# Query rows and output rows with the weights as moving operand, in a decode-attention and GLU backward kernel

## The chip, the cores and the metric

The kernel runs on one core of one Trainium2 chip. The metric is the device time of one execution in microseconds (us). A kernel's number is the median of several executions; executions of one kernel mostly lie within 0.3% of each other. A profile is one of these executions with the hardware profiler's records; its "span", from the first to the last instruction, is about 1.8 us shorter than the time. Engines are written PE (tensor engine; PEld is its weight load), DVE (vector), ACT (scalar), POOL (GpSimd) and SP (the queue that issues the large transfers). The granted clock is the share of its full clock that PE got, the DMA share the mean busy share of the 16 DMA engines; PSUM is the memory that PE writes its sums to.

## The reference

The program is one decode step, one token, with 32 heads and a cache of 8192 positions, plus a gated MLP, and the gradient of all of it. Cut to what matters:

```python
def _fwd_reference(A_x, A_k_cache, A_v_cache, A_wq, A_wo, B_x, B_w1, B_w3, B_w2):
    # x is 1 x 640; K and V are 32 heads x 8192 x 128; F of the MLP is 1728
    xn = _layernorm(x)
    q = xn @ wq                       # 4096 = 32 heads x 128
    p = softmax(q . k * Dh**-0.5)
    o = p . v
    return x + o @ wo + (silu(xn @ w1) * (xn @ w3)) @ w2

def reference(..., grad_out):
    _out, _vjp = jax.vjp(_f, A_x, A_k_cache, A_v_cache, A_wq, A_wo, B_w1, B_w3, B_w2)
    return (_out, *_vjp(grad_out))    # out_0, and out_1 = dx, dK, dV, dwq, dwo, dw1, dw3, dw2
```

K and V are read once (134 MB together) and gradients of the same size are written once. Nearly all the rest is the weights and their gradients. Each byte is used in a handful of operations.

## The kernel before

Heads are worked in groups of four (`GH = 4`), with one load of `wq` and `wo` per group. The 2 MB blocks of K and V live in ten buffers. A gradient is written into the buffer of the block that it belongs to, stored, and the buffer then takes a new load:

```python
    def store(kind, h):
        t = kv_tiles.pop((kind, h))
        ...
        fifo((dkc if kind == "K" else dvc)[h], t[:])    # 2 MB store on the SP queue
        free_slots.append(t)
        load_next()                                     # the next 2 MB load, into a freed buffer
```

These are the parts that the change touches. First q of a group, as columns: the weights are the stationary operand and one column of `xn` moves, 20 matmuls of one column.

```python
    def prep_q(g, ps, first):
        for hh in range(GH):
            for ci in range(NC):                        # NC = 5 blocks of 128 rows of D = 640
                nc.tensor.matmul(ps[:, hh:hh + 1], lhsT=G_["wq"][:, ci, hh * DH:(hh + 1) * DH],
                                 rhs=xn_col_bf[:, ci:ci + 1], ...)
        nc.scalar.activation(G_["cb"][:, 0, :], ps, ACTF.Copy, scale=scale)
```

Then the sum for `out_0`, again with the weights stationary: 20 matmuls of one column for each group, and 70 in the MLP (14 blocks of F by 5). The dx sum of the MLP lies in the same PSUM bank, `acc`, until the end.

```python
    acc = ps_acc.tile([P, 512], F32, name="acc")
    dx_acc = acc[:, 0:NC * RX].rearrange("p (c r) -> p c r", r=RX)
    OUT0 = NC * RX
    ...                                                 # fin_pe(g), once per group
            for ci in range(NC):
                nc.tensor.matmul(acc[:, OUT0 + ci:OUT0 + ci + 1], lhsT=G_["wo"][:, hh, ci * P:(ci + 1) * P],
                                 rhs=G_["od_bf"][:, hh, 0:1], ...)
    ...                                                 # mlp(), once, before head 2
            for ci in range(NC):
                nc.tensor.matmul(acc[:, OUT0 + ci:OUT0 + ci + 1], lhsT=wsrc[0:rows, ci * P:(ci + 1) * P],
                                 rhs=hcol_bf[0:rows, b:b + 1], ...)
    ...                                                 # the broadcasts of the MLP's gradient rows come next
    ...                                                 # the end
    nc.vector.tensor_reduce(dxm[:], dx_acc, AX.X, ALU.add)
    nc.vector.tensor_tensor(fin[:, 0:NC], acc[:, OUT0:OUT0 + NC], x_col[:], ALU.add)
    ...                                                 # fin is transposed, cast and stored by four small DMAs
```

## Time and profile before

| what | before | where it is read |
|---|---|---|
| time | 732.5 us, 732.12 to 733.51 in 3 runs | runs |
| span of the profile | 730.6 us | head of the page |
| PE, DVE, ACT busy | 83%, 63%, 51% | part 1 |
| moved | 303.58 MB, 416 GB/s on average | DMA line |
| matmuls (each with its weight load) | 5669 | part 1 |

The strips show what no average tells: the DMA engines are at 9 tenths or more in all slices but the last. The chain of work that ended last, by engine, looks otherwise:

```profile
PE 42%; DMA 41%; DVE 8%; ACT 6%; issue 1%; SPq 0%; ACTq 0%; DVEq 0%
```

This chain follows, at each step, whatever released the step last. A store frees a buffer, a load fills it, the tensor engine works on it, a store leaves: the walk passes through compute on a path that lies beside a full DMA pipe.

### The profile page before, as it was taken

What the parts mean: (1) busy time and instruction counts of PE and PEld (TensorE: products, weight loads), DVE (VectorE), ACT (ScalarE), POOL (GpSimd) and SP (SyncE); (2) the same over time, 40 slices, a digit from 0 to 9 for tenths busy, and PEclk for the clock granted to TensorE, in tenths of its full rate; (3) what the DMA queues carried; (4) which work ended last, traced back from release to release, by engine and by line L of the source; (5) the groups of instructions that cost most, each with busy time, mean ns of one, the idle gap of its engine ahead of it and who ended that gap; (6) DMA issues with size and microseconds to landing.
All of it is one profiled execution on the core that took longest, in us unless ns stands there. A gap on an engine that the chain in (4) does not pass through costs nothing.

```text
span 730.6 us, 13869 instructions
## 1 busy us (share of the span) xinstructions
PE 606.6 (83%) x5669; PEld 423.1 (58%) x5669; DVE 459.3 (63%) x806; ACT 369.4 (51%) x719; POOL 29.9 (4%) x45
## 2 busy tenths in 40 slices
PE   3989589998899889988987887888898889978940
PEld 2657466666566656666655555566566556655620
DVE  4069646677757776776646765547756756667482
ACT  2650736656556556554655554545554536655510
POOL 0010110000100000001000000000000000000000
PEclk9996699999999999988998998979897969989765
DMA  9999999999999999999999999999999999999993
GB/s 354 400 411 420 425 421 432 415 429 425 417 416 426 429 427 421 430 428 426 425 428 426 431 423 427 429 428 428 427 424 429 429 427 428 428 434 426 425 393 155
DMA packets 27145, 303.58 MB, mean 416 GB/s; under 512 B 2807, under 2 KB 4153, under 8 KB 10441
## 3 DMA queue, kind: packets, MB, share of 16 engines
q1 hardware_dynamic: 21328, 276.39, 89.5%
q0 software_dynamic: 5728, 26.30, 8.9%
q8 instruction: 44, 0.72, 0.4%
q14 instruction: 21, 0.16, 0.1%
q10 hardware_dynamic: 24, 0.01, 0.0%
HBM read 151.34 MB, written 151.34 MB: 414 GB/s over the span
## 4 chain that ended last, share of the span: by engine, by line
PE 42%; DMA 41%; DVE 8%; ACT 6%; issue 1%; SPq 0%; ACTq 0%; DVEq 0%
DMA out_dram<-kv 22%; PE pT L305 20%; DMA kv<-in_A_k_cache_dram 11%; DMA kv<-in_A_v_cache_dram 7%; PE m L340 6%; PE X L417 5%; ACT KT L307 4%; PE sA L324 4%; DVE kv L450 3%; PE dA L324 2%; DMA wo_g<-in_A_wo_dram 2%; DVE side L251 1%; PE gu_ps L527 1%; ACT KT L330 1%; PE m L430 1%
## 5 line engine op out<-in xcount | busy, mean ns | idle before, releaser
L307 ACT COPY KT<-pT 128x512 f32<-128x512 f32 x512 | 289.5, 589 | 235.3 <-PE pT L305 200.6
L305 PE MATMUL pT<-ident_f,kv 128*128 128x128 f32 x2048 | 318.7, 296 | 40.6 <-DMA kv<-in_A_k_cache_dram 17.9
L305 PEld LDWEIGHTS pT<-ident_f,kv 128*128 128x128 f32 x2048 | 248.5, 154 | 97.0 <-PE pT L305 27.8
L450 DVE TENSOR_TENSOR kv<-qd,U 128x4096 bf16<-128x4096 bf16 x64 | 146.0, 2284 | 0.0
L450 DVE TENSOR_TENSOR kv<-qd,P 128x4096 bf16<-128x4096 bf16 x64 | 143.6, 2284 | 0.0
L340 PEld LDWEIGHTS m<-selc,KT 128*128 128x128 f32 x512 | 67.4, 205 | 45.8 <-ACT KT L330 34.1
L340 PE MATMUL m<-selc,KT 128*128 128x16 f32 x512 | 73.2, 276 | 22.7 <-ACT KT L330 22.5
L417 PE MATMUL X<-kv,Z 128*32 128x512 bf16 x1024 | 85.3, 462 | 1.8 <-DVE Z L434 1.8
L400 DVE SCALAR_TENSOR_TENSOR U<-m,P 128x64 bf16<-128x64 f32 x32 | 7.4, 233 | 104.9 <-PE m L340 104.9
L324 PE MATMUL dA<-KT,qz 128*32 128x512 bf16 x512 | 55.2, 418 | 0.2 <-ACT KT L307 0.2
L324 PE MATMUL sA<-KT,qz 128*32 128x512 bf16 x512 | 55.1, 421 | 0.0
L324 PEld LDWEIGHTS <-qz 128*32 128x32 bf16 x1024 | 26.6, 93 | 42.8 <-issue 41.6
L417 PEld LDWEIGHTS <-Z 128*32 128x32 bf16 x1024 | 28.6, 110 | 33.9 <-issue 16.6
L366 DVE TENSOR_REDUCE mrow<-m 128x1 f32<-128x64 f32 x32 | 7.1, 223 | 62.9 <-PE m L340 62.9
L360 ACT CAST qd<-pT 128x256 bf16<-128x256 f32 x32 | 11.9, 372 | 48.6 <-DVE kv L450 32.4
L500 DVE SCALAR_TENSOR_TENSOR wq_g<-wq_g,side 128x512 bf16<-128x512 bf16 x40 | 27.3, 683 | 0.0
L251 DVE SCALAR_TENSOR_TENSOR side<-wo_g,g_bc 128x640 bf16<-128x640 bf16 x32 | 26.2, 819 | 1.1 <-DMA wo_g<-in_A_wo_dram 0.8
L373 DVE TENSOR_REDUCE negM<-m 128x1 f32<-128x128 f32 x32 | 9.3, 291 | 24.5 <-PE m L370 24.5
L432 DVE SCALAR_TENSOR_TENSOR U<-m,P 128x128 bf16<-128x128 f32 x32 | 11.4, 355 | 18.0 <-PE m L430 18.0
L390 DVE RECIPROCAL rZ<-m 128x1 f32<-128x1 f32 x32 | 5.3, 167 | 24.1 <-PE m L384 24.1
L330 ACT COPY KT<-dA 128x512 f32<-128x512 f32 x32 | 19.3, 604 | 0.6 <-PE dA L324 0.6
L330 ACT COPY KT<-sA 128x512 f32<-128x512 f32 x32 | 19.3, 603 | 0.0
(154 smaller groups left out, 365.2 us busy)
## 6 DMA issues: line engine op xcount, KB each, us to landing
out_dram<-kv SPq DMA_DIRECT2D x64, 2048.0 KB, 31.1
kv<-in_A_k_cache_dram SPq DMA_DIRECT2D x32, 2048.0 KB, 25.2
kv<-in_A_v_cache_dram SPq DMA_DIRECT2D x32, 2048.0 KB, 26.3
out_dram<-wo_g POOLq DMA_DIRECT2D x8, 640.0 KB, 11.4
out_dram<-wq_g POOLq DMA_DIRECT2D x8, 640.0 KB, 12.9
wq_g<-in_A_wq_dram POOLq DMA_DIRECT2D x7, 640.0 KB, 13.2
wo_g<-in_A_wo_dram POOLq DMA_DIRECT2D x7, 640.0 KB, 19.3
kv<-in_B_w_dram SPq DMA_DIRECT2D x2, 1728.0 KB, 28.7
```

Source lines behind the costliest of these rows:

```text
L251: nc.vector.scalar_tensor_tensor(junk[:], G_["wo"][:, hh, :], 1.0, g_bc[:], ALU.mult, ALU.mult, accum_out=G_["do"][:, hh:hh + 1])
L305: nc.tensor.transpose(pT[:, k * P:(k + 1) * P], W3[:, 4 * c + k, :], ident_f[:])
L307: nc.scalar.copy(KT[:].rearrange("p k w -> p (k w)"), pT[:])
L324: nc.tensor.matmul(S_[kind][q:q + QW, :], lhsT=S_["qz"][:, o:o + QW], rhs=KTb[:, par, :], start=(c0 == 0), stop=(c0 == NCH - 2), skip_grou ...
L330: nc.scalar.copy(XS[:].rearrange("p k w -> p (k w)"), S_.pop(kind)[:])
L340: nc.tensor.matmul(S_["m"][:, b0:b0 + J].rearrange("p (c k t) -> p k c t", k=4, t=2)[:, k, :, :], lhsT=XS[:, k, :], rhs=selc[:].rearrange( ...
L360: nc.scalar.copy(qd[:].rearrange("p a d -> p (a d)"), hd[h].pop("ps_r"))
L373: nc.vector.tensor_reduce(S_["negM"][:], S_["m"][:, 2 * J:2 * J + P], AX.X, ALU.max, negate=True)
L417: nc.tensor.matmul(xg["X"][q:q + QW, :], lhsT=Z[:, o:o + QW], rhs=W[:, N4 * i:N4 * (i + 1)], start=(slot == 0 and i < 4), stop=(slot == NS ...
L432: nc.vector.scalar_tensor_tensor(S_["U2"][:], S_["V"][:, 0:J].unsqueeze(2).to_broadcast([P, J, 2]), S_["m"][:, OC + NS:OC + NS + 1], S_["P ...
L450: nc.vector.tensor_tensor(dst[:, lo * DH:hi * DH].rearrange("p (j a b) -> p j a b", a=DH // 2, b=2), vec.rearrange("p (a b) -> p a b", b=2 ...
L500: nc.vector.scalar_tensor_tensor(wq_g[:, ci, :], wq_g[:, ci, :], 1.0, dqb, ALU.mult, ALU.mult, accum_out=dxa[:, ci, g:g + 1])
```

## The change

The intent was fewer and wider matmuls. The weights become the moving operand, 512 or 320 columns at a time, and a broadcast vector is stationary. `q` and `out_0` then come out as rows. Five wide matmuls and four one-column ones replace 20 for q, and 8 replace 20 for `out_0` per group; the MLP's 70 become 28 plus six that add `x`. dx of the MLP moves to a bank of its own and is reduced at once, the MLP's small vectors move into an unused tail of a buffer, and `out_0` leaves as two row stores. The core of the diff:

```diff
-    dx_acc = acc[:, 0:NC * RX].rearrange("p (c r) -> p c r", r=RX)
-    OUT0 = NC * RX
+    DHALF = D // 2
+
+    def out_row(vec, mat):
+        k = mat.shape[0]
+        for e in range(2):
+            nc.tensor.matmul(acc[64 * e:64 * (e + 1), 0:DHALF], lhsT=vec.to_broadcast([k, 64]),
+                             rhs=mat[:, e * DHALF:(e + 1) * DHALF], start=False, stop=True, skip_group_check=True)
...
-    def prep_q(g, ps, first):
+    def prep_q(g):
         G_ = grp[g]
+        pq = pst()
+        for ci in range(NC):
+            nc.tensor.matmul(pq[:], lhsT=xn_col_bf[:, ci:ci + 1].to_broadcast([P, P]), rhs=G_["wq"][:, ci, :],
+                             start=(ci == 0), stop=(ci == NC - 1))
+        G_["qrow"] = t_tile()
+        nc.scalar.activation(G_["qrow"][0:1, 0:GW], pq[0:1, :], ACTF.Copy, scale=scale)
+
+    def prep_qc(g, ps, first):
+        G_ = grp[g]
+        qrow = G_.pop("qrow")
         for hh in range(GH):
-            for ci in range(NC):
-                nc.tensor.matmul(ps[:, hh:hh + 1], lhsT=G_["wq"][:, ci, hh * DH:(hh + 1) * DH], ...)
-        nc.scalar.activation(G_["cb"][:, 0, :], ps, ACTF.Copy, scale=scale)
+            nc.tensor.matmul(ps[:, hh:hh + 1], lhsT=qrow[0:1, hh * DH:(hh + 1) * DH], rhs=one_bf[0:1, :], ...)
+        nc.scalar.copy(G_["cb"][:, 0, :], ps)
...
-            for ci in range(NC):
-                nc.tensor.matmul(acc[:, OUT0 + ci:OUT0 + ci + 1], lhsT=G_["wo"][:, hh, ci * P:(ci + 1) * P], ...)
+            out_row(G_["od_bf"][:, hh, 0:1], G_["wo"][:, hh, :])
...
+            out_row(hcol_bf[0:rows, b:b + 1], wsrc[0:rows, :])      # the MLP; then six matmuls that add x
...
+        dx_acc = ps_d.tile([P, NC, RX], F32, name="dx_acc", tag="dA")
...
+        nc.vector.tensor_reduce(dxm[:], dx_acc[:], AX.X, ALU.add)  # at the end of mlp()
...
+    row_bf = t_tile()[:, 0:DHALF]
+    nc.vector.tensor_copy(row_bf, acc[:, 0:DHALF])
+    out_0v = out_0.rearrange("a b (e c) -> (a b e) c", e=2)
+    for e in range(2):
+        nc.scalar.dma_start(out_0v[e:e + 1, :], row_bf[64 * e:64 * e + 1, :])
```

More of the change, by code (lines that the diff above doesn't have):

```diff
@@ L254, in prep_do @@
             nc.vector.tensor_copy(G_["cb"][:, 1, :], G_["do"][:])
-    def prep_q(g, ps, first):
+    def prep_q(g):
         G_ = grp[g]
-        for hh in range(GH):
-            for ci in range(NC):
-                nc.tensor.matmul(ps[:, hh:hh + 1], lhsT=G_["wq"][:, ci, hh * DH:(hh + 1) * DH],
-                                 rhs=xn_col_bf[:, ci:ci + 1], start=(first and hh == 0 and ci == 0),
-                                 stop=(ci == NC - 1), skip_group_check=True)
-        nc.scalar.activation(G_["cb"][:, 0, :], ps, ACTF.Copy, scale=scale)
+        pq = pst()
[7 more added lines that the diff above has]
+        qrow = G_.pop("qrow")
+        for hh in range(GH):
+            nc.tensor.matmul(ps[:, hh:hh + 1], lhsT=qrow[0:1, hh * DH:(hh + 1) * DH], rhs=one_bf[0:1, :],
+                             start=(first and hh == 0), stop=True, skip_group_check=True)
+        nc.scalar.copy(G_["cb"][:, 0, :], ps)
     def prep_sel(g, ps):
@@ L486, in fin_pe @@
         for hh in range(GH):
-            for ci in range(NC):
-                nc.tensor.matmul(acc[:, OUT0 + ci:OUT0 + ci + 1], lhsT=G_["wo"][:, hh, ci * P:(ci + 1) * P],
-                                 rhs=G_["od_bf"][:, hh, 0:1], start=False, stop=True, skip_group_check=True)
+            out_row(G_["od_bf"][:, hh, 0:1], G_["wo"][:, hh, :])
     def fin_wo(g):
@@ L519, with mt @@
     blocks_f = [(b, min(P, F - b * P)) for b in range(NB)]
-    hcol = consts.tile([P, NB], F32, name="hcol")
+    mt_f = mA[:, NA * F:].bitcast(F32)
+    mt_at = [0]
+    def mt(cols):
+        r = mt_f[:, mt_at[0]:mt_at[0] + cols]
+        mt_at[0] += cols
+        return r
+    hcol = mt(NB)
     def mlp():
@@ L546, in mlp @@
                                  start=False, stop=True, skip_group_check=True)
-        gu = consts.tile([P, 2, NB], F32, name="gu")
-        nc.vector.memset(gu[:], 0.0)
+        gu = mt(2 * NB).rearrange("p (w b) -> p w b", w=2)
+        nc.vector.memset(gu, 0.0)
         nc.vector.tensor_copy(gu[:, :, 0:NFULL], gu_ps[:, :, 0:NFULL])
@@ L553, in mlp @@
         up = gu[:, 1, :]
-        dhc = consts.tile([P, NB], F32, name="dhc")
-        nc.vector.tensor_reduce(dhc[:], dh_ps[:], AX.X, ALU.add)
-        sig = consts.tile([P, NB], F32, name="sig")
-        nc.scalar.activation(sig[:], gate, ACTF.Tanh, scale=0.5)
-        nc.vector.tensor_scalar(sig[:], sig[:], 0.5, 0.5, ALU.mult, ALU.add)
-        silu = consts.tile([P, NB], F32, name="silu")
-        nc.vector.tensor_tensor(silu[:], gate, sig[:], ALU.mult)
-        nc.vector.tensor_tensor(hcol[:], silu[:], up, ALU.mult)
@@ L562, in mlp @@
-        hcol_bf = consts.tile([P, NB], BF16, name="hcol_bf")
-        nc.vector.tensor_copy(hcol_bf[:], hcol[:])
-        dgu = consts.tile([P, 2, NB], F32, name="dgu")
-        nc.vector.tensor_tensor(dgu[:, 1, :], dhc[:], silu[:], ALU.mult)
-        t1 = consts.tile([P, NB], F32, name="t1")
-        nc.vector.tensor_scalar(t1[:], sig[:], -1.0, 1.0, ALU.mult, ALU.add)
-        nc.vector.tensor_tensor(t1[:], t1[:], gate, ALU.mult)
-        nc.vector.tensor_scalar(t1[:], t1[:], 1.0, None, ALU.add)
@@ L570, in mlp @@
-        nc.vector.tensor_tensor(t1[:], t1[:], sig[:], ALU.mult)
-        nc.vector.tensor_tensor(dgu[:, 0, :], dhc[:], up, ALU.mult)
-        nc.vector.tensor_tensor(dgu[:, 0, :], dgu[:, 0, :], t1[:], ALU.mult)
-        dgu_bf = consts.tile([P, 2, NB], BF16, name="dgu_bf")
-        nc.vector.tensor_copy(dgu_bf[:], dgu[:])
+        dhc = mt(NB)
+        nc.vector.tensor_reduce(dhc, dh_ps[:], AX.X, ALU.add)
+        sig = mt(NB)
+        nc.scalar.activation(sig, gate, ACTF.Tanh, scale=0.5)
+        nc.vector.tensor_scalar(sig, sig, 0.5, 0.5, ALU.mult, ALU.add)
@@ new lines, in mlp @@
+        silu = mt(NB)
+        nc.vector.tensor_tensor(silu, gate, sig, ALU.mult)
+        nc.vector.tensor_tensor(hcol, silu, up, ALU.mult)
+        hcol_bf = mt(NB // 2).bitcast(BF16)
+        nc.vector.tensor_copy(hcol_bf, hcol)
+        dgu = mt(2 * NB).rearrange("p (w b) -> p w b", w=2)
+        nc.vector.tensor_tensor(dgu[:, 1, :], dhc, silu, ALU.mult)
+        t1 = mt(NB)
+        nc.vector.tensor_scalar(t1, sig, -1.0, 1.0, ALU.mult, ALU.add)
+        nc.vector.tensor_tensor(t1, t1, gate, ALU.mult)
@@ L575, in mlp @@
+        nc.vector.tensor_scalar(t1, t1, 1.0, None, ALU.add)
+        nc.vector.tensor_tensor(t1, t1, sig, ALU.mult)
+        nc.vector.tensor_tensor(dgu[:, 0, :], dhc, up, ALU.mult)
+        nc.vector.tensor_tensor(dgu[:, 0, :], dgu[:, 0, :], t1, ALU.mult)
+        dgu_bf = mt(NB).bitcast(BF16).rearrange("p (w b) -> p w b", w=2)
+        nc.vector.tensor_copy(dgu_bf, dgu)
         for b, rows in blocks_f:
             wsrc = w2a[:, b, :] if b < NBA else w2b[:, b - NBA, :]
-            for ci in range(NC):
-                nc.tensor.matmul(acc[:, OUT0 + ci:OUT0 + ci + 1], lhsT=wsrc[0:rows, ci * P:(ci + 1) * P],
-                                 rhs=hcol_bf[0:rows, b:b + 1], start=False, stop=True, skip_group_check=True)
+            out_row(hcol_bf[0:rows, b:b + 1], wsrc[0:rows, :])
@@ new lines, in mlp @@
+        x_cb = mt(4).bitcast(BF16)[:, 0:NC]
+        nc.vector.tensor_copy(x_cb, x_col[:])
+        for ci in range(NC):
+            for e in range(2):
+                lo, hi = max(ci * P, e * DHALF), min((ci + 1) * P, (e + 1) * DHALF)
+                if lo < hi:
+                    nc.tensor.matmul(acc[64 * e:64 * (e + 1), lo - e * DHALF:hi - e * DHALF],
+                                     lhsT=x_cb[:, ci:ci + 1].to_broadcast([P, 64]),
+                                     rhs=ident_bf[:, lo - ci * P:hi - ci * P], start=False, stop=True,
+                                     skip_group_check=True)
@@ L605, in mlp @@
                 nc.scalar.copy(bc_sb[:, wi, f0:f1], pb[:, 0:f1 - f0])
+        dx_acc = ps_d.tile([P, NC, RX], F32, name="dx_acc", tag="dA")
+        nc.vector.memset(dx_acc[:], 0.0)
         FA, FB = 256, 832
@@ L633, in mlp @@
         load_next()
+        nc.vector.tensor_reduce(dxm[:], dx_acc[:], AX.X, ALU.add)
+    dxm = consts.tile([P, NC], F32, name="dxm")
     gate = consts.tile([P, 1], F32, name="gate")
@@ L674, in side_pe1, with side_pe1b @@
         elif hh == 3 and g + 1 < NG:
-            prep_q(g + 1, hd[h]["m"][:, 320:320 + GH], False)
+            prep_q(g + 1)
+    def side_pe1b(h):
+        g, hh = divmod(h, GH)
+        if hh == 3 and g + 1 < NG:
+            prep_qc(g + 1, hd[h]["m"][:, 320:320 + GH], False)
     def side_pe2(h):
@@ L732, in head @@
         T(h, "V", 7)
+        side_pe1b(h)
         Mp(h, "V", 4)
@@ L762 @@
     ps_0 = pst()
-    prep_q(0, ps_0[:, 0:GH], True)
+    prep_q(0)
+    prep_qc(0, ps_0[:, 0:GH], True)
     for hh in range(GH):
@@ L786 @@
         fin_wq(NG - 1, ci)
-    fin = consts.tile([P, 2 * NC], F32, name="fin")
-    dxm = consts.tile([P, NC], F32, name="dxm")
-    nc.vector.tensor_reduce(dxm[:], dx_acc, AX.X, ALU.add)
+    fin = consts.tile([P, NC], F32, name="fin")
     dxn = consts.tile([P, NC], F32, name="dxn")
@@ L793 @@
     nc.vector.tensor_tensor(dxn[:], dxn[:], dxm[:], ALU.add)
-    nc.vector.tensor_tensor(fin[:, 0:NC], acc[:, OUT0:OUT0 + NC], x_col[:], ALU.add)
+    row_bf = t_tile()[:, 0:DHALF]
+    nc.vector.tensor_copy(row_bf, acc[:, 0:DHALF])
+    out_0v = out_0.rearrange("a b (e c) -> (a b e) c", e=2)
+    for e in range(2):
+        nc.scalar.dma_start(out_0v[e:e + 1, :], row_bf[64 * e:64 * e + 1, :])
     st = consts.tile([P, 2], F32, name="st")
@@ L805 @@
     nc.vector.tensor_scalar(t5[:], t5[:], nst[:, 0:1], rstd[:], ALU.add, ALU.mult)
-    nc.vector.tensor_tensor(fin[:, NC:2 * NC], t5[:], g_col[:], ALU.add)
+    nc.vector.tensor_tensor(fin[:], t5[:], g_col[:], ALU.add)
     ps_o = pst()
-    nc.tensor.transpose(ps_o[0:2 * NC, 0:P], fin[:], ident_f[:])
-    fin_bf = consts.tile([2 * NC, P], BF16, name="fin_bf")
-    nc.vector.tensor_copy(fin_bf[:], ps_o[0:2 * NC, 0:P])
-    for dst, r0, cuts in ((out_0, 0, (0, 3, 5)), (out_1, NC, (0, 4, 5))):
-        for lo, hi in zip(cuts, cuts[1:]):
-            nc.scalar.dma_start(dst.rearrange("a b (c p) -> (a b c) p", p=P)[lo:hi, :], fin_bf[r0 + lo:r0 + hi, :])
+    nc.tensor.transpose(ps_o[0:NC, 0:P], fin[:], ident_f[:])
+    fin_bf = consts.tile([NC, P], BF16, name="fin_bf")
+    nc.vector.tensor_copy(fin_bf[:], ps_o[0:NC, 0:P])
+    nc.scalar.dma_start(out_1.rearrange("a b (c p) -> (a b c) p", p=P), fin_bf[:])
 _INS = ['A_x', 'A_k_cache', 'A_v_cache', 'A_wq', 'A_wo', 'B_x', 'B_w1', 'B_w3', 'B_w2', 'grad_out']
```

## The prediction

> **What bounds the kernel now.** I read the strips of 40 slices first, because they show whether one resource is full throughout.
>
> ```profile
> PE   3989589998899889988987887888898889978940
> PEclk9996699999999999988998998979897969989765
> DMA  9999999999999999999999999999999999999993
> GB/s 354 400 411 420 425 421 432 415 429 425 417 416 426 429 427 421 430 428 426 425 428 426 431 423 427 429 428 428 427 424 429 429 427 428 428 434 426 425 393 155
> ```
>
> The 16 DMA engines are busy in every slice but the last and move an even 415 to 434 GB/s from the fourth slice to the 38th. The tensor engine is busy too, but its digits wander; nothing holds it at a fixed rate. The table by windows (window, busy us of each engine, granted clock, DMA share, GB/s) gives the sizes:
>
> ```profile
> 0.00:20.00 20.00, 7.67 (x62) 5.97 (x63) 7.65 (x37) 6.40 (x11) 0.69 (x6) 1.00 0.92 358
> 20.00:40.00 20.00, 18.54 (x165) 12.79 (x164) 4.77 (x12) 12.77 (x24) 1.88 (x3) 0.91 1.01 400
> ...
> 300.00:400.00 100.00, 87.59 (x771) 61.55 (x770) 65.89 (x107) 52.25 (x106) 3.26 (x4) 0.88 1.01 427
> ...
> 700.00:710.00 10.00, 3.09 (x36) 2.82 (x32) 9.18 (x11) 1.33 (x3) 0.00 (x0) 0.50 0.96 410
> 710.00:720.00 10.00, 0.93 (x3) 0.59 (x3) 6.76 (x27) 0.00 (x0) 1.63 (x2) 0.50 0.85 346
> 720.00:731.00 11.00, 0.00 (x0) 0.00 (x0) 0.00 (x0) 0.00 (x0) 0.00 (x0) 0.50 0.08 34
> ```
>
> The span follows from this. 303.58 MB at the 427 GB/s of the middle take 711 us. The start loses about 5 us (the first 20 us at 358 cost 3.2, the next 40 us at 400 and 413 cost 2). The last 31 us move 4.1 + 3.5 + 0.4 = 7.9 MB, worth 18.6 us, so they lose 12.4. With 1 us from 650 to 700 that is about 729.5, against a span of 730.6. To be faster a change must move fewer bytes or shorten start or end.
>
> The last 11 us hold no engine work at all, and a DMA share of 0.08, about one engine of 16. The completion records in the trace show why: each 2 MB transfer lands in 16 parts, and one part comes later and later than the one before it: 0.5 us late near 290 us, 3 near 440, 6 near 640, 9 for the last stores. That engine works without a gap to 729.5 us, while the others are done by about 722. The waits of the issuing queue agree:
>
> ```profile
> SPq L105 <- DMA out_dram<-kv: 470.1, 53, 17.1
> SPq L105 <- DVE kv L450: 102.4, 16, 12.3
> ...
> SPq L839 <- DMA out_dram<-fin_bf: 11.6, 1, 11.6
> ```
>
> The queue mostly waits for earlier stores to land, which frees the buffer of the next load. The wait at the end is put down to the small output, but in the packet records that output is through by about 720.4 us; what still runs are 16 KB packets of the large stores.
>
> **How much room compute has.** A head moves 8.39 MB of K, V and their gradients and 0.66 MB of wq and wo traffic, 21.2 us at 427 GB/s. From 330 us on, heads are 21.3 us apart (times of the negM reductions); from 163 to 236 us, where compute sets the pace, four take 72.4 us, 18.1 each. So a group of four heads has 12.4 us of slack.
>
> **What the Trainium skill says.** "DMA: Bandwidth & Descriptors", section "Where 436 GB/s comes from", gives 435.2 GB/s as the ceiling of the 16 DMA ports; this trace runs at 427, 98% of it, and agrees. "Runtime: NRT & Kernel Launch", section "Instruction fetch mechanics", says that instructions arrive by DMA in 16 KiB blocks of 256. The trace agrees: the instruction queue q8 has 44 packets and 0.72 MB, and 2 x 5669 tensor instructions are 44.3 blocks. "TensorE: Matmul & The Clock Gate", section "Back-to-back issue gap", gives N/2.4 + 2.5 ns for a warm matmul of N columns, 216 ns for 512. The trace has 20 matmuls of 384 columns in 5.06 us at a clock near 0.67, or 253 ns each, so I use 0.22 to 0.34 us for 512.
>
> **The change part by part.** These are the rows it touches:
>
> ```profile
> L488 PE MATMUL acc<-od_bf,wo_g 128*128 128x1 bf16 x160 | 5.2, 164 | 0.0
> L260 PE MATMUL m<-xn_col_bf,wq_g 128*128 128x1 bf16 x140 | 4.5, 163 | 3.2 <-DVE rZ L390 3.2
> L578 PE MATMUL acc<-hcol_bf,kv 128*128 128x1 bf16 x65 | 1.8, 163 | 1.4 <-DVE hcol_bf L563 1.4
> ```
>
> Because they overlap, I take stretches of the timeline: 20 of them run in 0.64 us, the 70 of the MLP in 1.97 us.
>
> 1. *q.* Per group, 20 narrow matmuls (0.64 us) become five of 512 columns (1.1 to 1.7) and four of one column (about 0.15): 0.6 to 1.2 us more. The row passes through the scalar engine (a 512-column copy took 0.59 us); the eight transposes placed between hide most of it, up to 0.6 us is left. It borrows one of three pT banks and one of four KT buffers for a moment.
> 2. *out_0 per group.* 20 narrow ones become 8 of 320 columns in two halves of the array. The X sums show that column strips run side by side: 16 matmuls of 512 columns in four strips took 1.27 us, 0.32 per round. A pair of 320 is then about 0.20, four pairs 0.8, against 0.64. With step 1 a group gains 0.8 to 2 us of tensor work, well inside 12.4.
> 3. *out_0 of the MLP.* 70 become 28 (14 pairs, 2.8 us) and six small ones for x (0.2): 1 us more at full clock, up to 3.5 at half clock. The broadcasts after it feed the scalar copies which the vector engine awaits at 81 us, so head 2 starts 1 to 3.5 us later. In the thin place behind the MLP, the store issued at 122.1 us should come before the first engine finishes the load ahead of it at 129.0; less 1.5 us of latency that leaves 5 us. So it stays hidden.
> 4. *Instruction count.* 390 load-and-matmul pairs go, 72 + 64 + 34 = 170 come: 440 instructions fewer, as the built order confirms (6279 to 5839 rows). That is 1.7 blocks of 16 KB. A fetch packet took 1.0 us and the packet after it often 1.0 instead of 0.61, so a block costs at most some 1.45 us of one engine: 2.5 engine-us, 0.16 us shared among 16, or up to 2.5 us if all fall on the engine that ends last. I take 0.5.
> 5. *The end.* The dx reduction (0.4 us on the chain) and the out_0 add (0.1) leave the final chain, a row copy of 320 columns (about 0.45) enters, one small store fewer is issued, and the vector engine waits up to 1 us longer for the tensor engine to have read wo. All lie beside the last DMA engine's 9 us of backlog: nothing.
> 6. *The start.* q of group 0 ends 1.5 us later, but the vector engine's do sums there end at 16.4 us against 13.1 for q: nothing. The dx bank is reduced before head 2 needs it.
>
> The sum is 0 - 0.5 - 0 = about -0.6 us on 732.5.
>
> **The rivals.** *A: compute becomes the bound.* Wide matmuls make the tensor engine, at 83% the busiest, slower. Between 100 and 286 us compute does set the pace and the DMA backlog is thin, so a delay above 5 us behind the MLP would idle all engines, 2 to 6 us on the total: 734 to 738. Against it: the issue-to-landing time there, median 16.7 us for transfers that need about 5, shows other transfers waiting. *B: the tail shrinks.* If instruction blocks fall mainly on the late engine, 2 to 3 us go: 729 to 730. For it: something does load that engine unequally. Against it: 44 blocks at 1.45 us all on it would make it 64 us late, not 9. *C: fewer instructions make heads faster and the kernel with them.* Tensor time per group does not fall by my count, and a faster head would wait for the same bytes; 718 us, 2% less, is below what 16 evenly loaded engines could reach with this start and end.
>
> **Range and chances.** The three runs before spread over 1.4 us. B gives the lower end, A the upper: 728.5 to 735.5, centre 731.8. Faster by 2% needs 14.6 us, more than the whole loss of the tail (0.01); slower by 2% needs a stall of 15 us that no step suggests (0.02); within 2% 0.97.
>
> **What would show it.** Right: the GB/s strip again 415 to 434, q8 with 42 or 43 packets, heads late in the run still 21.3 us apart, a last stretch of 7 to 11 us with a DMA share near one engine and no engine work. Step 2 is wrong if the two halves run one after the other (over 1.1 us for eight); step 3 if head 2 starts over 4 us later or a slice near 130 us falls below 400 GB/s. The prediction is wrong if the last engine's delay changes by more than 3 us, or if the DMA engines run dry after the MLP.

## The result

The changed kernel took 733.64 us (median of 6 runs, 732.56 to 734.57), and the kernel before on the same chip 732.96 us (6 runs, 731.86 to 733.97). The ratio is 1.0009, 95% interval 0.9994 to 1.0024: the same. A ratio is the mean time of one kernel's runs over that of the other's of the same rounds, so it is not quite the ratio of the medians quoted. Repeated later on another chip, the changed kernel took 732.74 against 733.72 us, ratio 0.9984 (0.9970 to 0.9998). The two comparisons differ in sign by about as much as each is wide. The change is worth nothing that these runs can tell from zero, and single differences of 1 us are not to be read.

The strips of the changed kernel's page (tenths per slice of 18.3 us, then GB/s):

```profile
DMA  9999999999999999999999999999999999999993
GB/s 349 397 411 419 428 421 428 393 427 425 427 420 426 431 426 424 426 430 425 429 422 430 427 425 426 426 430 429 425 428 428 431 424 433 429 425 426 422 401 136
```

The DMA row is what it was. Only the eighth slice, around 137 us, is new: 393 GB/s, against 415 before (412 in the repeat). The windows of the changed kernel (start and end, length, busy us of PE, PEld, DVE, ACT and POOL with instruction counts, granted clock, DMA share, GB/s) put sizes to the strip:

```profile
120.00:140.00 20.00, 19.17 (x185) 13.34 (x182) 15.61 (x24) 12.90 (x26) 0.00 (x0) 1.00 1.00 406
140.00:160.00 20.00, 19.14 (x174) 13.24 (x173) 13.90 (x22) 11.53 (x24) 0.76 (x1) 0.91 1.00 411
710.00:720.00 10.00, 0.93 (x3) 0.58 (x3) 6.98 (x27) 0.00 (x0) 1.63 (x2) 0.50 0.86 351
720.00:732.00 12.00, 0.00 (x0) 0.00 (x0) 0.00 (x0) 0.00 (x0) 0.00 (x0) 0.50 0.11 47
```

The first two stretches in the kernel before:

```profile
120.00:140.00 20.00, 18.63 (x197) 13.27 (x193) 15.68 (x24) 12.53 (x28) 0.00 (x0) 1.00 1.01 421
140.00:160.00 20.00, 18.87 (x187) 12.91 (x183) 13.82 (x21) 11.80 (x24) 0.76 (x1) 0.91 1.00 423
```

The end is the old one: no engine work after 720 us and a DMA share of 0.11, one to two engines of 16. From 120 to 160 us the changed kernel moved 15 and 12 GB/s less, which is 27 × 20 / 427 = 1.3 us worth of transfer. That looks like the cost of the change. The repeat had 417 and 420 GB/s there, so half or more of the 1.3 us is the difference between two executions of one kernel. The experiments deal with this place.

The waits of the issuing queue in the changed kernel:

```profile
SPq L105 <- DMA out_dram<-kv: 412.4, 50, 16.2
SPq L105 <- DVE kv L464: 143.3, 21, 13.4
SPq L878 <- DMA out_dram<-wq_g: 12.1, 1, 12.1
```

The queue still mostly waits for stores to land and then for the DVE's gradients; the shares move about between executions (469.1 and 101.5 us in the repeat). The end wait is now put down to another small store, with the same 12 us. The name has changed and the wait has not: what lasts are the packets of the large stores.

What the tensor engine does for q can be read from the timeline of the changed kernel around 208 us (start, duration, engine, line and operation; in brackets its idle time before and who ended it):

```profile
207.63 1.24 PE L266 MATMUL pT<-wq_g,xn_col_bf 128*128 128x512 bf16 x5
...
208.97 0.59 ACT L269 ACTIVATE KT<-pT 1x512 bf16<-1x512 f32 x1 [0.96 <-PE pT L266]
...
209.61 0.25 PE L275 MATMUL m<-one_bf,KT 1*128 1x1 bf16 x4 [0.30 <-ACT KT L269]
```

Five wide matmuls take 1.24 us. The first is 0.378 us long (the median of this line's matmuls), so each further one adds (1.24 − 0.378) / 4 = 0.216 us, the 216 ns that the prediction quotes for a warm matmul of 512 columns. The row copy is hidden but for 0.30 us of PE waiting. At 147.91 us, in the same timeline, the eight `out_row` matmuls of a group take 0.73 us.

The MLP's 70 narrow matmuls, in the timeline before, and the 28 that take their place with those for x, the first broadcast copy and the vector engine's start after:

```profile
71.72 1.97 PE L578 MATMUL acc<-hcol_bf,kv 128*128 128x1 bf16 x70 [1.43 <-DVE hcol_bf L563]
...
74.06 6.91 ACT L600 CAST kv<-pT 128x512 bf16<-128x512 f32 x3 [3.70 <-PE pT L596]
...
81.00 1.90 DVE L613 TENSOR_TENSOR KT<-kv,kv 128x1024 bf16<-128x1024 bf16 x3 [3.91 <-ACT kv L600]
```

```profile
72.36 2.21 PE L199 MATMUL acc<-kv,kv 128*64 128x320 bf16 x28 [1.43 <-DVE kv L583]
...
74.50 0.34 PE L604 MATMUL acc<-ident_bf,kv 128*64 128x128 bf16 x6
...
75.20 6.90 ACT L628 CAST kv<-pT 128x512 bf16<-128x512 f32 x3 [4.57 <-PE pT L624]
...
82.14 2.50 DVE L643 TENSOR_TENSOR KT<-kv,kv 128x1024 bf16<-128x1024 bf16 x4 [3.94 <-ACT kv L628]
```

A pair of halves takes (2.21 − 0.30) / 13 = 0.147 us after the first. Scaled from the 0.216 us for 512 columns, one matmul of 320 would take 0.135 us and two one after the other 0.27: the two 64-column halves run side by side. The DVE starts 1.14 us later than before (82.14 against 81.00), but 0.64 us of that were there already when the rows began (72.36 against 71.72). The MLP's rows themselves add 2.21 + 0.34 − 1.97 = 0.58 us.

At the end the dx reduction is gone from the final chain and a copy of the row is in it. The timeline of the changed kernel there:

```profile
715.44 0.48 DVE L832 CAST KT<-acc 128x320 bf16<-128x320 f32 x1
...
718.32 0.28 DVE L851 CAST fin_bf<-pT 5x128 bf16<-5x128 f32 x1 [0.56 <-PE pT L849]
```

Before, the last cast started at 718.11. The chain is no shorter, and the last DMA engine works 11 to 13 us past it in both kernels (to 729.6 and 731.0 us in the completion records).

### The profile page after: what moved, and what is told of

Its sections match the earlier page's. It is cut to its first block, busy times and chain, and to the rows that moved or that the text cites. A ratio compares the mean times of both kernels' runs of the same rounds, so it can differ in the third digit from the quotient of the medians.

```text
span 732.0 us, 13418 instructions
## 1 busy us (share of the span) xinstructions
PE 619.7 (85%) x5449; PEld 426.8 (58%) x5449; DVE 460.9 (63%) x808; ACT 372.8 (51%) x727; POOL 29.9 (4%) x45
## 3 DMA queue, kind: packets, MB, share of 16 engines
HBM read 151.34 MB, written 151.34 MB: 413 GB/s over the span
## 4 chain that ended last, share of the span: by engine, by line
DMA 46%; PE 36%; DVE 7%; ACT 5%; SPq 2%; issue 1%; ACTq 0%; DVEq 0%
DMA out_dram<-kv 26%; PE pT L319 17%; DMA kv<-in_A_k_cache_dram 11%; DMA kv<-in_A_v_cache_dram 10%; PE m L354 6%; PE X L431 4%; DVE kv L464 4%; ACT KT L321 4%; PE sA L338 3%; PE dA L338 2%; SPq L105 1%; PE m L398 1%; ACT E L393 1%; ACT KT L344 1%; PE m L444 1%
## 5 line engine op out<-in xcount | busy, mean ns | idle before, releaser
L319 PEld LDWEIGHTS pT<-ident_f,kv 128*128 128x128 f32 x2048 | 250.5, 155 | 87.0 <-PE pT L319 29.8
L354 PEld LDWEIGHTS m<-selc,KT 128*128 128x128 f32 x512 | 69.7, 211 | 46.0 <-ACT KT L344 36.1
L354 PE MATMUL m<-selc,KT 128*128 128x16 f32 x512 | 75.8, 281 | 22.8 <-ACT KT L344 22.6
L414 DVE SCALAR_TENSOR_TENSOR U<-m,P 128x64 bf16<-128x64 f32 x32 | 7.4, 232 | 101.5 <-PE m L354 101.5
```

Source lines behind the costliest of these rows:

```text
L319: nc.tensor.transpose(pT[:, k * P:(k + 1) * P], W3[:, 4 * c + k, :], ident_f[:])
L354: nc.tensor.matmul(S_["m"][:, b0:b0 + J].rearrange("p (c k t) -> p k c t", k=4, t=2)[:, k, :, :], lhsT=XS[:, k, :], rhs=selc[:].rearrange( ...
```

## The experiments

Twelve runs were made: ten new kernels, the changed kernel again and one of the ten again. Kernels are compared only within the same rounds. The prediction held, so these runs ask whether it held for its reasons. The theory is that bytes and the tail set the time, that compute is hidden, and that some few us are lost or won only behind the MLP (near 130 us) and at the end. The rivals are that two real effects cancelled; that the number of instructions, through their fetches, matters; and that the tail is something a kernel can shorten.

### Half of the change each

*q rows alone* is the kernel before with this edit and the two calls that belong to it:

```diff
-    def prep_q(g, ps, first):          # 20 one-column matmuls
+    def prep_q(g):                     # 5 x 512 columns, row copy
+    def prep_qc(g, ps, first):         # 4 one-column matmuls
```

> The kernel before with only the q part of the change (rows of q with the weights moving). Theory 'DMA and one late engine': the time stays within 0.3% of before, late heads stay 21.3 us apart, the last engine still ends some 8 us after the others. Rival 'cancellation' (one part helps, the other hurts, the sum is nil): this part alone moves the time by over 0.5% in one direction and the other part alone by as much in the other.

*out_0 rows alone* is the changed kernel with q put back:

```diff
-    def prep_q(g):
-    def prep_qc(g, ps, first):
+    def prep_q(g, ps, first):          # as before
```

> The changed kernel with the q part undone, so only the out_0 rows, the own bank for dx and the new ending. 'DMA and one late engine': within 0.3% of before; head 2 starts 1.3 us later than before, as in the changed kernel, which costs at most about 1 us of transfer behind the MLP. 'Cancellation': over 0.5% away from before, on the other side than the q part alone.

q rows alone took 733.21 us and out_0 rows alone 733.03 us, against 733.06 us before; both ratios are 0.9998, with intervals of 0.9984 to 1.0012 and 0.9984 to 1.0013. There was no cancellation of two effects larger than about 1 us: each half is nothing by itself. The expectation for out_0 rows alone had one miss: head 2, which should have started 1.3 us later than before, started at 110.26 us against 110.28.

### More tensor instructions, and more tensor time

*48 small matmuls per head* adds 3072 instructions (1536 load-and-matmul pairs) to the changed kernel, into unused columns of `acc`:

```diff
         side_pe1(h)
         T(h, "V", 7)
         side_pe1b(h)
+        for _ in range(48):
+            nc.tensor.matmul(acc[:, 400:401], lhsT=ident_bf[:], rhs=one_bf[:], start=False, stop=True,
+                             skip_group_check=True)
```

> The changed kernel plus 48 needless one-column matmuls in every head: 3072 more tensor instructions, 12 more instruction blocks of 16 KB, some 1.5 us of tensor time per head, which fits the 3 us of slack. If instruction blocks spread over all 16 engines at 1.45 us each: 12 x 1.45 / 16 = 1.1 us more. If they fall on the late engine: up to 17 us more. If compute sets the time: 32 x 1.5 = 48 us more. I hold the first or close to nothing, because in the two traces the packets that delay the late engine are those of the other engines' instruction queue, not of the tensor engine's.

*18 matmuls of 192 columns per head* is meant to take about the same tensor time with fewer instructions:

```diff
+        for _ in range(18):
+            nc.tensor.matmul(acc[:, 320:512], lhsT=ident_bf[:], rhs=g_bc[:, 0:192], start=False, stop=True,
+                             skip_group_check=True)
```

> The same tensor time in fewer instructions: 18 needless matmuls of 192 columns in every head, about 1.5 us per head, 1152 more instructions, 4.5 more blocks. If only bytes and the late engine count: within 0.3% of the changed kernel, below e3 by 0.7 us if blocks spread, by up to 11 us if they fall on the late engine. If tensor time sets the pace: about 48 us more, like e3.

The first took 737.54 us (ratio 1.0056, interval 1.0040 to 1.0071), the second 735.16 us (1.0028, 1.0012 to 1.0043), before being 733.06 us. In the first one's timeline 40 of the 48 take 1.14 us, so a head got about 1.4 us more tensor work; in the second one's the 18 take 1.65 us. Over 32 heads that is about 44 and 53 us, and the kernels lost 4 and 2 us. That is how little PE's part of the chain meant. (PE's busy time in sum is a poorer measure. It rose by 19 and 22 us over the changed kernel's first profile, at a higher mean granted clock, but the changed kernel's own two profiles, 619.7 and 602.4 us, are 17 us apart.) The instruction queue of the first experiment's page, and the windows where it lost:

```profile
q8 instruction: 55, 0.90, 0.5%
```

```profile
120.00:140.00 20.00, 19.63 (x223) 14.03 (x223) 13.65 (x24) 11.16 (x23) 0.00 (x0) 1.00 0.88 344
140.00:160.00 20.00, 19.87 (x238) 14.48 (x241) 13.07 (x23) 13.00 (x26) 0.76 (x1) 1.00 1.00 421
```

The same stretches of the second:

```profile
120.00:140.00 20.00, 19.63 (x199) 13.45 (x201) 14.50 (x25) 11.94 (x25) 0.00 (x0) 1.00 0.97 388
140.00:160.00 20.00, 19.88 (x203) 14.42 (x196) 13.17 (x21) 12.03 (x24) 0.76 (x1) 1.00 1.00 414
```

The DMA share falls to 0.88 and 0.97 there; in the first one's strip the slice around 119 us is the only one below nine tenths before the last. Weighed against the 427 GB/s of the middle, the first loses (83 + 6) × 20 / 427 = 4.2 us in these 40 us and the second (39 + 13) × 20 / 427 = 2.4, where the kernel before loses (6 + 4) × 20 / 427 = 0.5. That is 3.7 us more than before for the first, whose runs are 4.1 us over before (its profiled execution 4.8), and 1.9 for the second, with 2.1 (its profiled execution 3.1). For twelve more fetched blocks (55 packets instead of 43) some 0.4 to 1.1 us remain, no more certain than a us or two. On the late engine alone twelve blocks at 1.45 us would have made 17 us. The stretch in which one engine works alone at the end was 6.6 us here, against 7.1 in the changed kernel and 7.2 before. Twelve more fetched blocks of tensor instructions did not lengthen the tail.

### The place behind the MLP

The prediction gave this place 5 us of margin. *Delay at the MLP* puts 55 matmuls of 192 columns ahead of the broadcasts, once:

```diff
+        for _ in range(55):
+            nc.tensor.matmul(acc[:, 320:512], lhsT=ident_bf[:], rhs=g_bc[:, 0:192], start=False, stop=True,
+                             skip_group_check=True)
         for wi in range(2):
             for b0 in range(0, NB, 4):
```

> The changed kernel with 55 needless matmuls of 192 columns ahead of the MLP's broadcasts, about 5 to 6 us of tensor time. My prediction said that the place behind the MLP has 5 us of margin: then the loss is below 1 us beyond the changed kernel. If the margin is already used up, as the traces of the changed kernel and of e3 suggest: nearly the whole delay is lost, 4 to 6 us more, with the 120 to 140 window near 300 to 340 GB/s, and the late engine as late as ever.

It took 735.96 us against 733.51, ratio 1.0034 (1.0019 to 1.0049). The first reduction of head 2's maximum (the start of the head's chain) in the changed kernel and then in this one:

```profile
111.57 0.29 DVE L387 TENSOR_REDUCE negM<-m 128x1 f32<-128x128 f32 x1 [0.81 <-PE m L384]
```

```profile
114.23 0.29 DVE L387 TENSOR_REDUCE negM<-m 128x1 f32<-128x128 f32 x1 [0.81 <-PE m L384]
```

And this kernel's windows:

```profile
120.00:140.00 20.00, 19.17 (x191) 13.08 (x194) 14.73 (x27) 12.33 (x25) 0.00 (x0) 1.00 0.91 362
140.00:160.00 20.00, 19.14 (x195) 13.31 (x187) 13.92 (x22) 12.52 (x27) 0.76 (x1) 1.00 1.00 418
```

Head 2 began 2.7 us later than in the changed kernel and 3.9 us later than before (110.28), under the 5 us that should have been free, and the DMA engines stood idle for 9% of 20 us. The loss by the windows is (65 + 9) × 20 / 427 = 3.5 us, 3.0 more than before, for a time 2.5 us longer. The loss is less than the 4 to 6 us expected for a margin already used up, and the window stayed above the 300 to 340 GB/s expected, but the margin is not 5 us: of 3.9 us of delay, 2.5 reached the time. How the price grows with the delay was not swept.

*MLP rows split* is the reverse: half of the row blocks, the x rows and the w2 store move behind the first three broadcast groups, so that head 2 starts earlier.

```diff
-        for b, rows in blocks_f:
-            out_row(hcol_bf[0:rows, b:b + 1], wsrc[0:rows, :])
-        ...                                # x rows, w2 gradient and its store
+        rows_of(blocks_f[:7])
         for wi in range(2):
             for b0 in range(0, NB, 4):
                 ...                        # one broadcast group
+                if wi == 0 and b0 == 8:
+                    rows_of(blocks_f[7:])
+                    ...                    # x rows, w2 gradient and its store
```

> The changed kernel with half of the MLP's out_0 rows and the x rows put behind the first three broadcast groups, so that the scalar copies start as early as before. If the changed kernel's 1.3 us later head 2 is what lets the DMA engines run short behind the MLP (406 and 411 GB/s from 120 to 160 us against 421 and 423 before): head 2 back within 0.3 us of before, the two windows back near 421, and about 1 us less than the changed kernel, so level with before or a little below. If that dip is chance: no change against the changed kernel and the dip stays.

It took 732.16 us against 733.51, ratio 0.9982 (0.9970 to 0.9994), with head 2 at 108.90 us and no loss to be seen in the windows:

```profile
120.00:140.00 20.00, 19.17 (x186) 13.42 (x182) 15.62 (x24) 13.03 (x28) 0.00 (x0) 1.00 1.00 417
140.00:160.00 20.00, 19.14 (x188) 13.47 (x185) 13.87 (x25) 13.00 (x27) 0.76 (x1) 1.00 1.02 430
```

That looked like a version that beats both kernels, so I ran it once more beside the changed kernel itself, on one chip.

> The changed kernel once more, beside the next run, so that the two are compared on one chip. Every theory: about 1.001 of the kernel before, within 0.998 to 1.003.

> The changed kernel with half of the MLP's out_0 row blocks, the x rows and the w2 store placed behind the first broadcasts of the first heads, once more. If the thin place at 120 to 160 us is what it cures, it is 0.7 to 1.5 us below the changed kernel in the same call and 0.997 to 0.9995 of the kernel before. If the earlier gain was chance, the two agree within 0.5 us.

The changed kernel took 732.74 us (ratio 0.9984, 0.9970 to 0.9998), the split 732.93 us (0.9988, 0.9975 to 1.0000), the kernel before 733.72 us. The two agree within 0.2 us in their medians (0.3 by the ratios), so the expectation's other branch came true: the split's earlier gain over the changed kernel is not confirmed. Its windows in this execution:

```profile
120.00:140.00 20.00, 19.17 (x184) 13.38 (x182) 15.60 (x24) 13.06 (x27) 0.00 (x0) 1.00 1.01 399
140.00:160.00 20.00, 19.14 (x188) 13.50 (x186) 13.91 (x22) 13.15 (x26) 0.76 (x1) 1.00 1.00 424
```

Head 2 began at 109.52 us here, earlier than in any execution of the changed kernel, and the first window still lost 28 GB/s. The profiles together, with the start of head 2, the loss counted as above, the time against before as (ratio − 1) × 733 us, and the time of the profiled execution itself less the median of before:

| kernel | head 2 at, us | GB/s 120 to 140, 140 to 160 us | loss, us | loss over before's, us | time over before, us | profiled execution over before, us |
|---|---|---|---|---|---|---|
| before | 110.28 | 421, 423 | 0.5 | 0 | 0 | −0.6 |
| q rows alone | 109.12 | 426, 425 | 0.1 | −0.4 | −0.1 | −0.4 |
| out_0 rows alone | 110.26 | 413, 423 | 0.8 | 0.3 | −0.1 | −0.1 |
| changed, first | 111.57 | 406, 411 | 1.7 | 1.2 | +0.7 | +0.8 |
| changed, repeat | 110.60 | 417, 420 | 0.8 | 0.3 | −1.2 | −1.0 |
| MLP rows split | 108.90 | 417, 430 | 0.3 | −0.2 | −1.3 | −1.0 |
| MLP rows split, repeat | 109.52 | 399, 424 | 1.5 | 1.0 | −0.9 | 0.0 |
| 18 matmuls of 192 columns | 111.51 | 388, 414 | 2.4 | 1.9 | +2.1 | +3.1 |
| delay at the MLP | 114.23 | 362, 418 | 3.5 | 3.0 | +2.5 | +1.2 |
| 48 small matmuls | 113.75 | 344, 421 | 4.2 | 3.7 | +4.1 | +4.8 |

For the last three, the loss agrees with the mean time within 0.5 us, but in part by luck: the loss is that of one execution, and with that execution's own time it agrees only within 1.1 to 1.8 us. The windows tell where the time is lost, and its size to a us or two. They also show what the times can't: by and large, the later head 2 starts, the larger the loss. Three runs below leave everything before head 8 as in the changed kernel and so are further samples of it here: head 2 at 110.78, 110.96 and 111.22 us, losses of 0.9, 1.6 and 1.1 us. With the two of the changed kernel and out_0 rows alone, the new MLP's loss is 0.8 to 1.7 us in six profiles, against 0.5 and 0.1 us in the two with the old one. So the change does seem to cost some 0.8 us in the thin place, but its times, +0.7 and −1.2 us, do not show it.

### The engine that ends last

Four runs looked for a way to shorten the last 7 us or for their cause. *Vector instructions* adds 48 tiny DVE memsets to each of heads 8 to 27, and *POOL instructions* 80 such on POOL, to raise the instruction fetches of other engines.

```diff
+        for _ in range(48 if 8 <= h < 28 else 0):
+            nc.vector.memset(tick[:], 0.0)
```

> The changed kernel with 48 needless one-element vector memsets in each of heads 8 to 27, where compute has slack: 960 more vector instructions, 7.5 fetch packets of 8 KB. In the trace the late engine's own delays follow 8 KB packets of queue q14 (0.31 us, and the packet after it takes 1.0 instead of 0.61). If those fetches all fall on the late engine: 7.5 x 0.76 = 5.7 us more at the end and a longer stretch with one engine alone. If they spread over 16 engines: 0.4 us. If the vector time matters: the heads after the eighth get further apart than 21.3 us.

```diff
+        for _ in range(80 if 8 <= h < 28 else 0):
+            nc.gpsimd.memset(tick[:], 0.0)
```

> The changed kernel with 80 needless one-element GpSimd memsets in each of heads 8 to 27: 1600 more instructions on an engine that is 4% busy and on nobody's path, so 12 to 13 more fetch packets of 8 KB and no compute time. This repeats the question of e6, whose memsets slowed the heads themselves. If those fetches fall on the late engine at 0.76 us each: 9 us more, with a longer stretch of one engine alone. If they fall on other engines or spread: 0 to 0.6 us.

The DVE run took 773.23 us against 733.51 (ratio 1.0577) and does not answer its question. Heads from 310 us on lay 23.4 us apart (310.33 to 685.19 us, 16 steps) instead of 21.2, the DMA engines were no longer full, and the lag of the late engine went down to 2 us or less. What it does show is the slack of a head. In one of these heads:

```profile
595.80 5.41 DVE L772 MEMSET tick<- 1x1 f32 x48
```

5.4 us more on the DVE's in-order queue put the heads 2.2 us further apart, so 3.2 us a head were hidden. That is the prediction's 12.4 us for a group of four, 3.1 a head. It also suggests that the lag builds only while the DMA engines are always full.

The POOL run took 736.86 us against 733.25 (1.0042, 1.0021 to 1.0064). POOL's instructions come through queue q14, as the DVE's do (27 packets in the DVE run). First the changed kernel's page, then this one's:

```profile
q14 instruction: 20, 0.16, 0.1%
```

```profile
q14 instruction: 32, 0.26, 0.1%
```

Twelve packets more, and in the completion records the late engine finished at 733.7 instead of 731.0 us, 2.7 us later. The stretch in which it works alone stayed at 7.0 us, but that stretch also hangs on when the other engines get their last work, and here the last head ended later (288 GB/s from 700 to 710 us). The lag itself, from the fifteenth to the sixteenth part of one large transfer, did grow:

| | before | changed | changed, repeat | 48 small matmuls | POOL instructions | range of the other full runs |
|---|---|---|---|---|---|---|
| mean lag of transfers that landed from 600 to 680 us, us | 5.6 | 6.1 | 5.7 | 4.4 | 9.1 | 3.3 to 6.7 |
| lag of the last store, us | 8.8 | 8.6 | 8.3 | 7.9 | 12.3 | 6.9 to 10.1 |

The last column holds those of the remaining runs whose DMA engines stayed full and whose completion records can be told apart (for the last store, without *tail split*). In the POOL run fifteen parts of the last store landed between 720.77 and 720.93 us and the sixteenth at 733.23. Some 3.5 us more for twelve packets is about 0.3 us for each, the time that one takes (0.31), where 0.76 was expected. So more POOL instructions make the late engine later; twelve more blocks of tensor instructions did not. This rests on one profile, and it does not separate the fetches from the memsets that they bring. What makes the rest of the lag stays open.

*Tail split* stores the last V gradient as 68 and 60 rows. "DMA: Bandwidth & Descriptors" of the Trainium skill, section "Why a DMA increments its semaphore by 16 and not by 1", says that a transfer is spread over the largest number of engines up to 16 that divides its slowest dimension on both sides, and that the lowest-numbered ones are taken on this kind of queue. 68 rows then go to four engines, and if the late one is not among them it gets less.

```diff
-        fifo((dkc if kind == "K" else dvc)[h], t[:])
+        cuts = (0, 68, P) if (kind, h) == ("V", H - 1) else (0, P)
+        for lo, hi in zip(cuts, cuts[1:]):
+            fifo((dkc if kind == "K" else dvc)[h][lo:hi, :], t[lo:hi, :])
```

> The changed kernel with the last V gradient stored as 68 rows and then 60 rows. By the skill's rule for the number of engines, 68 rows go to four engines, the lowest-numbered, and 60 rows to 15. In the changed kernel the late engine wrote one of the five rows of out_1 but none of the rows of the small outputs before, which used four engines at most, so it should be the fifth. Then it sheds four 16 KB packets, about 2.4 us, and the four others take 13 more, 7.9 us, on engines that stand idle by 720 us: 2 to 2.5 us less than the changed kernel. If the late engine is one of the first four: 5 us or more slower. If the end does not hang on the late engine: no change.

The trace agrees with the page: the 68 rows landed in four parts, at 719.5, 720.1, 720.9 and 724.9 us. The late engine finished the store before that only at 720.2 and could not have written 17 packets of 0.61 us by any of these times, so it is not among the four. But the time was 738.01 us against 733.51 (1.0064, 1.0052 to 1.0077), a miss. Windows of this run:

```profile
710.00:720.00 10.00, 0.93 (x3) 0.58 (x3) 6.23 (x24) 0.00 (x0) 1.22 (x2) 0.50 0.91 289
720.00:735.40 15.40, 0.00 (x0) 0.00 (x0) 0.00 (x0) 0.00 (x0) 0.00 (x0) 0.50 0.27 105
```

After 720 us a share of 0.27, about four engines, works to the end. The four that took the 68 rows became the late ones: a quarter of a store on each is more than the lag that was to be made up.

*Rows split with finer tail* cuts the last three large stores into 112 rows and four times four, on top of the MLP split:

```diff
+        late = h == H - 1 or (kind, h) == ("K", H - 2)
+        cuts = (0, 112, 116, 120, 124, P) if late else (0, P)
```

> The kernel of e7 with the last three 2 MB stores cut into 112 rows and four pieces of four rows. By the skill's rule 112 rows go to 16 engines, seven each, and four rows to the four lowest-numbered engines, one each. In e9 the four loaded engines wrote their 68 rows by 725.0 us, while the late engine had only finished the store before at 720.3, so the late engine is not one of the four, and e9 failed because the four got too much. Here the late engine sheds three 16 KB packets (1.8 us) and the four take nine more each (5.5 us): 1 to 1.8 us less than e7. If small pieces cost more than they shift, or the end hangs on something else: no gain or a loss.

It took 745.87 us against 733.25 (1.0164, 1.0136 to 1.0193), a clear miss. Its windows:

```profile
700.00:710.00 10.00, 4.05 (x34) 2.86 (x28) 8.88 (x7) 1.34 (x3) 0.00 (x0) 0.53 0.67 233
710.00:720.00 10.00, 1.46 (x7) 0.58 (x3) 7.95 (x30) 0.00 (x0) 1.63 (x2) 0.50 0.54 146
```

The last stores were issued too slowly for the engines: the queue's timeline has 12 issues in 25.78 us from 710.09 on, so the last one left only at about 736 us. The queue's waits in the trace tell why: from 690 us on it waited 21.0 us in four waits for earlier large stores to land and 7.0 us in two for the stores of `out_0`. A piece takes over the semaphore of an earlier transfer and first waits until that one has landed whole: the issues at 702.85, 710.09 and 715.27 us follow such a landing within 0.03 us. A store's last part is the late engine's, so these pieces waited for the engine that they were to relieve. The six runs lie in two groups, 742.7 to 743.7 and 748.0 to 748.3 us; the profile is of the first. No tail that I tried is better than the plain one.

## Why the prediction was right, and where not

The time was right: 731.8 us predicted, with 728.5 to 735.5, against 733.64 and 732.74 us measured.

- **The bound was right.** Some 44 and 53 us of added tensor work that cost 4 and 2 us, most of it in one thin place, are the direct proof; the unchanged DMA strip of the changed kernel agrees, and the DVE run measured the slack of a head at 3.2 us where 3.1 were predicted. That an earlier finish inside a head has nothing to give follows from this and was not run.
- **Step 1, right.** 1.1 to 1.7 us for the five wide matmuls: 1.24. About 0.15 for the four narrow: 0.25. Up to 0.6 left of the copy: 0.30.
- **Step 2, right.** 0.8 us for eight half matmuls: 0.73 at full clock, with the two halves side by side.
- **Step 3, right in the MLP's own cost, wrong in what follows from it.** 28 matmuls took 2.21 us where 2.8 were estimated, x took 0.34 where 0.2 was, 0.58 us more than the 70 narrow ones. Head 2 came 1.3 us later in the first profile (111.57 against 110.28), 0.3 later in the repeat and no later with out_0 rows alone, against 1 to 3.5 predicted: this term was too large. The failed step is "that leaves 5 us. So it stays hidden"; by the prediction's own sign for it, a slice near 130 us below 400 GB/s, the first profile with its 393 already said so (the repeat, with 412, did not). A delay of 3.9 us over before made the kernel 2.5 us longer, where it should have cost nothing. The 5 us came from one store's issue and the engine that finishes the load ahead of it. That single pair does not say when the other 15 engines run out. Nor does the median landing time of 16.7 us that the prediction sets against rival A, which is that of 100 to 200 us alone (29.8 from 200 to 300): the thin place has the shorter queue. In the packet records from 118 to 152 us, 23 of 792 packets of 16 KB on the SP queue already took over 0.7 us in the kernel before (0.61 is normal; from 300 to 334 us it is 4 of 844), 65 of 758 in the changed kernel, 38 of 778 in its repeat and 72 of 745 with the delay. I read this as engines running short of queued work even before the change, which the runs do not prove packet by packet. The prediction came out right all the same because the change's own delay is about 1 us or less and its price no larger than the spread between executions: two errors, a delay put too large and a margin put too large, met in a small loss, which is luck. Rival A, with its 2 to 6 us for a delay above 5, had the right mechanism: 3.9 us already cost 2.5.
- **Step 4, right in the count (44 to 43 packets), not confirmed in value.** The 0.5 us gain cannot be seen, and if twelve blocks cost 0.4 to 1.1 us for all, 1.7 blocks fewer are worth at most some 0.15 us, by this estimate. The term that was too large is the share on the late engine, whose lag twelve more blocks did not raise (7.9 us in the last store against 8.6). Rival B, a shorter tail through fewer blocks, falls with it.
- **Step 5, right.** The final chain is no shorter, the last cast starts at 718.32 instead of 718.11, and nothing depends on it.
- **Step 6, right in what ends last, wrong in a size.** In the changed kernel's trace q of group 0 is ready at 15.61 us, 2.5 later than before (13.12) and not 1.5, and the cast of do, at 16.70, still ends last. q rows alone, which change the start, made no difference of more than 1 us.
- **Rival C** falls: from the first maximum after 310 us to the last one, heads are 21.2 us apart before (310.07 to 692.10 us, 18 steps), 20.6 in the changed kernel (320.70 to 692.14, 18 steps) and 21.1 in its repeat, and the last head is reached within 1 us of the same moment in all three.

Still open is why one DMA engine falls behind steadily under full load. More tensor instruction fetches did not make it later; more POOL instructions did, by some 3.5 us, so POOL's fetches are likely a part of it, but not shown to be the whole.

## What to carry to other kernels

When all DMA engines are full from end to end, as here, ask of a compute change two things first: whether it moves fewer bytes, and whether it moves work into one of the few places where the queue of transfers is short. Find such a place by putting a few us of dummy work into it. The wait of one transfer is not its margin. And repeat a gain of 0.2% beside its nearest rival before you believe it: here the changed kernel was 1.0009 of the kernel before in one call and 0.9984 in the next.

## What the Trainium skill lacked or had wrong

- "DMA: Bandwidth & Descriptors", "Where 436 GB/s comes from", says without a condition that for transfers between HBM and SBUF the HBM side binds at about 358 GB/s per core, and in the next sentence has a measurement of 425. For one core at work the second is what these runs show: of 151.34 MB read and 151.34 MB written, the stretches from 160 to 690 us ran at 424 to 431 GB/s, 427 in the middle. The sentence lacks the condition that both cores of a pair are at work, which no run here tests.
- "Runtime: NRT & Kernel Launch", "Instruction fetch mechanics", calls the cost of a 16 KiB block mostly hidden and speaks only of the engine that fetches. It does not say that the packet takes 1.0 us of a data engine and costs it up to 1.45 us with the packet after. On a full pipe twelve tensor blocks still made only some 0.4 to 1.1 us, uncertain by a us or two. The fetches of POOL came as about 8 KB packets (0.26 MB in 32), a size that the section does not give.
- "DMA: Bandwidth & Descriptors", "Latency and other measured facts", says that two engines, 7 and 15, are usually slower, with no size. No page has it that one engine falls steadily behind when all 16 are always full: 0.5 us at 290 us, 3 at 440, 6 at 640 and about 9 at the end, and 12.3 with 1600 more POOL instructions. The lag fell to 2 us or less in the run whose DMA engines were not always full. The trace has no engine numbers. The late engine took one of the five rows of out_1 (in the changed kernel, landed at 723.69 us, the other four by 720.29) but none of the 68 rows that went to four engines, so by the same page's rule for HWDGE it would be the fifth, not 7 or 15, if it is the same one in both runs.
